# First loads, unread products and weight conversion re-ordered, and the last sums moved, in a fused retention and feed-forward kernel

## The chip, the cores and the metric

The kernel runs on one core of a Trainium2 chip. The metric is the device time in microseconds (us) of one execution, lower is better. The times given are medians of several executions; one further execution was taken with the hardware profiler on, and all rows of a profile below are from such an execution.

## The reference: what is computed

Inputs are q, k and v of shape (8 batches, 8 heads, 576 tokens, 64), in float32, and two weight matrices of 64-bit floats: w_in (512 x 2048) and w_out (2048 x 512). The output is float32, 4608 x 512.

```
scores = q @ k.T / sqrt(64)
ret    = scores * gamma_h ** (i - j)   where i >= j, else 0     (gamma_h = 1 - 2 ** (-5 - h))
attn   = ret @ v                       # per batch and head
x      = attn, heads side by side      # 4608 tokens x 512
h      = max(x @ w_in, 0)
out    = (h * h) @ w_out
```

## The kernel before, in words

**Retention.** Tokens are taken in 40 chunks, five to a batch: four of 128 tokens and one of 64. For a chunk, `turn` (L375) transposes q and k on TensorE (PE) and copies the results out with ScalarE (ACT, k) and VectorE (DVE, q); `scores` (L396) makes the products of q and k on PE, masks them on DVE (`ret`), and lets GpSimd (POOL) scale v by the decay. `retain_a`, `retain_b` and `retain_c` (L443 to L500) then make the output of the chunk and a running state u that one chunk hands to the next; the finished x of the chunk is copied by ACT into `xT`. POOL also scales the q of chunks 1 to 3 (`scale_q`, L370), in program order with the v's.

**Loads.** `load(i)` (L131) issues q, k and v of chunk i on SyncE's queue (SP): q and k in three transfers each, v in one. Chunks 0 to 2 are loaded ahead; turn i of the main loop (L708) then calls `load(i + 3)`, and in turns 0 to 3 `fetch_raw(1)` behind it, which loads one piece of w_in. One more piece is loaded ahead of the loop.

**Weight conversion.** The chip gets w_in as 64-bit words. A piece is 128 of its columns, 16 pieces in all. `round_parts` (L200) turns one into float32 in six steps: `one` and `two` on DVE (L209, L213), `beside`, two activations on ACT (L217, L218), then `three`, `four`, `five` on DVE (L221, L224, L227). The generator `w_in_parts` (L292) hands the steps out in this order: `one` and `two` of piece 0; then for each piece j: `beside` of j, `one` and `two` of j + 1, `three`, `four`, `five` of j. So six steps make one piece. `convert(n)` (L313) emits the next n steps at the place in the program where it is called; there is no scheduler, each engine runs what it is given in the order of the program.

**First block.** The feed-forward part takes 512 tokens as a block, nine in all. In block 0 the first matrix product is a plain one, `first_in(j)` (L545): four PE products of piece j with `xT` of block 0 (L553), then on ACT a ReLU of the result (L557), later a squaring on DVE (L560). `first_in(0)` and `first_in(1)` are called in turn 4 of the main loop; after that `ffn` (L668) calls three per chunk: in its first half `convert(6)` and one `first_in`, in its second half one `first_in`, `convert(6)`, another `first_in`, `convert(6)`. Blocks 1 to 8 use seven products in place of eight (`ffn_in`, L573), and from there PE has work waiting all the time.

**Unread products.** `warm` (L695) gives PE products whose results nobody reads.

**Second product.** When all tokens are through the first product, the loop over `inner` and `outer` (L824, L857) makes the second: 63 inner steps (9 blocks of 7 products), each of them again seven products of 128 x 128. DVE adds these up into `r`, and `outer` adds `r` into one or two quarters of the output and writes a half of it out when it is complete.

Of the kernel before, what the change touches and what calls it, by code (L numbers as in the profile page):

```python
# [9 lines left out]
F32 = mybir.dt.float32  # L10
# [3 lines left out]
ALU = mybir.AluOpType  # L14
# [3 lines left out]
TOK = 512  # L18
HT = TOK // 2
# [21 lines left out]
def kernel(  # L41
# [33 lines left out]
    nc = tc.nc  # L75
    ctx.enter_context(tc.manual_schedule())

    B, H, S, D = q.shape
# [9 lines left out]
    N_BLK = n_tok // TOK  # L88
    NP = len(PRODUCTS)
    NCH = -(-S // C)  # L90
    chunks = [(b, ci, ci * C, min(C, S - ci * C)) for b in range(B) for ci in range(NCH)]
    N_CH = len(chunks)
# [7 lines left out]
    ld3 = first.enter_context(tc.tile_pool(name="ld3", bufs=3))  # L100
    ld4 = first.enter_context(tc.tile_pool(name="ld4", bufs=4))
# [26 lines left out]
    loaded = {}  # L128
    N_EARLY = TOK // C

    def load(i):  # L131
        b, ci, c0, cs = chunks[i]
        got = {name: pool.tile([128, H, D], F32, tag=name, name=f"{name}_ld") for name, pool in (("q", ld3), ("k", ld4), ("v", ld4))}
        if i == 0:
            nc.sync.dma_start(dv, decay_v)
        if N_EARLY <= i < N_EARLY + NCH:

            nc.sync.dma_start(dq[:, :, c0:c0 + cs], decay_q[:, :, c0:c0 + cs])
        for name, src in (("q", q), ("k", k), ("v", v)):
            t = got[name]  # L140

            issue = nc.scalar if i == 0 and name != "q" else nc.sync
            at = src[b, :, c0:c0 + cs, :].rearrange("h s d -> s h d")
            if name == "v":
                issue.dma_start(t[:cs], at)
            else:

                issue.dma_start(t[:cs, 0:H // 2, :], at[:, 0:H // 2, :])
                for e in range(2):
                    issue.dma_start(t[:cs, H // 2 + e::2, :], at[:, H // 2 + 1 - e::2, :])  # L150
        loaded[i] = [got["q"], got["k"], got["v"]]

# [38 lines left out]
    def fetch_w(j):  # L193
        if j < len(pieces) and wide:
            nc.sync.dma_start(raw_of(j).bitcast(I64).rearrange("p (c f) -> p c f", c=N_DM), piece_src(j))
# [88 lines left out]
    def fetch_raw(count):  # L284

        for _ in range(count):
            if n_raw[0] < min(N_W1, n_made[0] + N_RAW):
                fetch_w(n_raw[0])
                n_raw[0] += 1
# [23 lines left out]
    def convert(count):  # L313
        for _ in range(count):
            f = next(w_in_steps, None)
            f and f()
# [4 lines left out]
    nc.gpsimd.memset(exp_bias, -896.0 * 2.0 ** 23)  # L321
    idle = only.tile([128, 128], F32, name="idle")
    nc.vector.memset(idle, 1.0)
    for i in range(3):
        load(i)
    fetch_raw(1)

    ident = only.tile([128, 128], F32, name="ident")
    make_identity(nc, ident)
# [3 lines left out]
    for half in range(2):  # L333
        at = slice(CH * half, CH * half + CH)
        nc.gpsimd.affine_select(
            out=msk[at, 0, 0, :], in_=msk[at, 0, 0, :], compare_op=ALU.is_ge, fill=0.0, base=0,
# [38 lines left out]
    def turn(i):  # L375

        cs, c0 = chunks[i][3], chunks[i][2]
        n_h = cs // CH
        p = ps_t.tile([128, 2, 512], F32, tag="t", name="t_ps").rearrange("p h (j d t) -> p h j d t", j=2, d=HP)
        for j in (1, 0):  # L380
            for hp in range(HP):
                for h in range(n_h):
                    nc.tensor.transpose(p[:, h, j, hp, :], loaded[i][j][rows(h), 2 * hp:2 * hp + 2, :],  # L383
                                        ident[rows(h), rows(h)])
        for j, name in ((1, "kT"), (0, "qT")):
            t = st[i][name] = work2.tile([128, HP, C], F32, tag=name, name=name) if j == 0 else work.tile([128, HP, C], F32, tag=name, name=name)
            to = t[:, :, :cs].rearrange("p d (h t) -> p h d t", h=n_h)
            if j:
                nc.scalar.copy(to, p[:, :n_h, j, :, :])
            elif i < N_EARLY:  # L390
                nc.vector.tensor_copy(to, p[:, :n_h, j, :, :])
            else:
                nc.vector.tensor_tensor(to, p[:, :n_h, j, :, :], dq[:, :, c0:c0 + cs].rearrange("p d (h t) -> p h d t", h=n_h),
                                        op=ALU.mult)
# [300 lines left out]
    def warm(count, wide):  # L695
        t = ps_f.tile([128, 512], F32, tag="f", name="idle_ps")
        for _ in range(count):
            if wide:
                nc.tensor.matmul(t[:, 0:128], lhsT=idle, rhs=idle, start=True, stop=True)
            else:  # L700
                for b in range(2):
                    nc.tensor.matmul(t[rows(b), 0:64], lhsT=idle[rows(0), rows(b)], rhs=idle[rows(0), 0:64], start=True, stop=True,  # L702
                                     skip_group_check=True)

    warm(6, True)
    scale_q(0, nc.vector)
    turn(0)
    for i in range(N_CH + 1):  # L708
        if i <= N_EARLY:

            convert((0, 0, 2, 5, 5)[i])
            if i >= 1:
                retain_a(i - 1)
                warm(4, False)
                retain_b(i - 1)
                warm(4, False)
                retain_c(i - 1)
            convert((0, 0, 1, 1, 1)[i])
            if i == N_EARLY:
                step()  # L720
            scores(i)
            if i == N_EARLY:
                convert(6)
                step()
            if i < N_EARLY:
                if i + 1 < N_EARLY:
                    scale_q(i + 1, nc.gpsimd)
                warm(6, False)
                turn(i + 1)
            else:  # L730
                convert(5)
        else:
            if i == N_EARLY + 1:
                gone[0] = TOK
            retain_a(i - 1)
            if i < N_CH:
                turn(i)
            ffn(i - 1, 0)
            retain_b(i - 1)
            if i < N_CH:  # L740
                scores(i)
            retain_c(i - 1)
            ffn(i - 1, 1)
        if i + 3 < N_CH:
            load(i + 3)
        if i < N_EARLY:
            fetch_raw(1)
    assert n_next[0] == N_BLK
# [15 lines left out]
    o_room = [part(at).rearrange("p (h j d) -> p h j d", h=2, j=2) for at in (7168, 9216)]  # L764
    N_K = N_BLK * NP
    BLOCKS = list(range(1, N_BLK)) + [0]
# [57 lines left out]
    def inner(k, i):  # L824

        n, j = divmod(k, NP)
        o = o_room[n % 2]
        if i == 0:
            small = late3.tile([128, 3, 128], F32, tag="small", name="small")
            r = o[:, 0, :, 0:HT] if j == 0 else late2.tile([128, 2, HT], F32, tag="r", name="r")  # L830
            state[k] = dict(r=r, lefts=lefts(k), p1=small[:, 0, :], u2=small[:, 1, :], p15=small[:, 2, :])
        s = state[k]
        left, right, to = PRODUCTS[i]
        if i in OPENS:
            s[to] = bank(f"o_{to}")
        p = s[to]
        for m in range(N_MQ):
            nc.tensor.matmul(p, lhsT=s["lefts"][left][:, m, :], rhs=w_out[j][:, m, WO_SLOT[right], :],  # L838
                             start=(i in OPENS and m == 0), stop=(i in CLOSES and m == N_MQ - 1),
                             skip_group_check=True)  # L840
        r = s["r"]
        if i == 0:
            nc.scalar.copy(s["p1"], p)
        elif i == 1:
            nc.vector.tensor_tensor(s["u2"], p, s["p1"], op=ALU.add)  # L845
        elif i == 2:
            nc.vector.tensor_tensor(s["p15"], p, s["p1"], op=ALU.add)
        elif i == 3:
            nc.scalar.copy(r[:, 0, 0:128], p)  # L849
        elif i == 4:  # L850
            nc.vector.tensor_tensor(r[:, 1, 128:], p, s["p15"], op=ALU.add)
        elif i == 5:
            nc.vector.tensor_tensor(r[:, 0, 128:], p, s["u2"], op=ALU.add)
        else:
            nc.vector.tensor_tensor(r[:, 1, 0:128], p, s["p1"], op=ALU.add)

    def outer(k):  # L857

        n, j = divmod(k, NP)
        r = state.pop(k)["r"]  # L860
        o = o_room[n % 2]
        c11, c12 = o[:, 0, :, 0:HT], o[:, 0, :, HT:]
        c21, c22 = o[:, 1, :, 0:HT], o[:, 1, :, HT:]
        for to, with_ in {1: [(c21, c11)], 2: [(c12, c21)], 3: [(c11, c11)], 4: [(c22, c12), (c21, c21)],
                          5: [(c12, c12)], 6: [(c21, c21)]}.get(j, []):
            nc.vector.tensor_tensor(to, r, with_, op=ALU.add)
        if j >= 5:
            half = j - 5
            row = BLOCKS[n] * TOK + half * HT
            nc.sync.dma_start(out[row:row + HT, :].rearrange("(a p) d -> p a d", p=128), o[:, half, :, :])  # L870
# [18 lines left out]
    for k in range(N_K + 1):  # L889
# [4 lines left out]
        for e in range(3):  # L894
# [8 lines left out]
            f = next(steps_0, None)  # L903
# [56 lines left out]
```

## Time and profile before

| What | us |
|---|---|
| median of 3 executions | 995.94 (995.22 to 996.46) |
| the profiled execution: its own time | 992.27 |
| the profiled execution: span from first to last instruction | 990.5 |
| PE busy | 974.3 (98% of the span) |
| DVE busy | 747.5 (75%) |
| ACT busy | 189.6 (19%) |
| POOL busy | 83.1 (8%) |
| first product of `first_in(0)` starts | 34.83 |
| last product of `first_in(15)` starts | 106.1 |
| last PE product ends | 985.6 |

Time in the profile counts from the start of the span. "PE" is the matrix product, "PEld" the loading of its stationary operand; a row of the timeline gives start, duration, engine, line, the tiles written and read with their sizes, how many instructions it merges, and in brackets how long the engine sat idle before it and what ended that.

### The profile page before, as it was taken

The numbers are of one execution on the slowest core, as the hardware profiler recorded it, in microseconds if no ns is written. First come the engines' busy times: TensorE is split into PE (matmuls) and PEld (weight loads), VectorE is DVE, ScalarE is ACT, GpSimd is POOL, SyncE is SP. The second block draws the span as 40 slices with busy tenths as digits, with TensorE's granted clock in tenths as the row PEclk, the third lists the DMA queues.
The fourth block names the chain that finished last, engine by engine and source line by source line (L and its number), as shares of the span: only waits on it lengthen the run. The fifth ranks groups of instructions, "written<-read, shape, count | busy, mean of one in ns | idle before, by whom it ended". The sixth has DMA issues, their size and how long they took to land.

```text
span 990.5 us, 24582 instructions
## 1 busy us (share of the span) xinstructions
PE 974.3 (98%) x10612; PEld 866.2 (87%) x10612; DVE 747.5 (75%) x1420; ACT 189.6 (19%) x459; POOL 83.1 (8%) x85
## 2 busy tenths in 40 slices
PE   7999999999999999999999999999999999999997
PEld 6645788888888888888888889999999999999997
DVE  2789797567878888888886777777777777776765
ACT  3455221112222222322211100000000000000000
POOL 3100011101112011110101000000000000000000
PEclk8999999999999999999999999999999999999999
DMA  8986647756796788779549999675583767556351
GB/s 190 262 235 174 184 148 200 199 139 182 206 302 215 200 261 240 219 231 269 160 180 330 406 382 349 233 268 171 214 296 138 258 207 274 192 190 237 116 202 43
DMA packets 187660, 220.40 MB, mean 223 GB/s; under 512 B 119200, under 2 KB 137632, under 8 KB 178592
## 3 DMA queue, kind: packets, MB, share of 16 engines
q1 hardware_dynamic: 185440, 218.31, 68.0%
q8 instruction: 83, 1.36, 0.6%
q10 hardware_dynamic: 2112, 0.52, 0.3%
q14 instruction: 25, 0.20, 0.1%
HBM read 129.41 MB, written 89.39 MB: 221 GB/s over the span
## 4 chain that ended last, share of the span: by engine, by line
PE 94%; DVE 4%; ACT 1%; issue 1%; DMA 0%; SPq 0%; DVEq 0%; ACTq 0%
PE o_b L838 17%; PE h_b L588 17%; PE o_c L838 11%; PE o_a L838 11%; PE h_c L588 11%; PE h_a L588 11%; PE h_ps L553 5%; PE x_ps L432 3%; PE t_ps L383 2%; PE x_ps L467 2%; PE sc_ps L411 2%; PE idle_ps L702 1%; PE u_ps L435 1%; DVE room L595 0%; DMA q_ld<-in_q_dram 0%
## 5 line engine op out<-in xcount | busy, mean ns | idle before, releaser
L588 PE MATMUL h_b<-room,w 128*128 128x256 f32 x736 | 177.2, 383 | 1.6 <-DVE room L516 0.9
L588 PEld LDWEIGHTS h_b<-room,w 128*128 128x128 f32 x736 | 137.2, 190 | 21.9 <-PE t_ps L383 1.1
L838 PE MATMUL o_b<-w,room 128*128 128x128 f32 x1168 | 144.5, 275 | 0.2 <-DVE room L789 0.2
L838 PEld LDWEIGHTS o_b<-w,room 128*128 128x128 f32 x1168 | 137.2, 192 | 0.5 <-DVE room L789 0.4
L838 PE MATMUL o_c<-w,room 128*128 128x128 f32 x1008 | 123.0, 275 | 0.0
L838 PEld LDWEIGHTS o_c<-w,room 128*128 128x128 f32 x1008 | 117.7, 192 | 0.0
L588 PE MATMUL h_c<-room,w 128*128 128x256 f32 x480 | 114.3, 381 | 0.0
L588 PE MATMUL h_a<-room,w 128*128 128x256 f32 x448 | 107.5, 383 | 0.0
L588 PEld LDWEIGHTS h_c<-room,w 128*128 128x128 f32 x480 | 90.5, 190 | 12.5
L588 PEld LDWEIGHTS h_a<-room,w 128*128 128x128 f32 x448 | 83.8, 190 | 11.8
L838 PE MATMUL o_a<-w,a 128*128 128x128 f32 x688 | 85.6, 275 | 0.0
L838 PEld LDWEIGHTS o_a<-w,a 128*128 128x128 f32 x688 | 81.2, 192 | 0.1
L605 POOL TENSOR_TENSOR room<-room 128x512 f32<-128x512 f32 x32 | 36.1, 1128 | 431.0 <-ACT room L604 361.6
L595 DVE SCALAR_TENSOR_TENSOR room<-room 128x512 f32<-128x512 f32 x96 | 67.5, 703 | 3.3
L849 ACT COPY r<-o_a 128x128 f32<-128x128 f32 x54 | 14.3, 265 | 276.9 <-PE o_a L838 246.4
L553 PE MATMUL h_ps<-room,w 128*128 128x512 f32 x128 | 58.1, 602 | 0.8 <-ACT room L489 0.7
L607 DVE TENSOR_TENSOR room<-h_b,room 128x512 f32<-128x512 f32 x32 | 22.1, 690 | 42.2 <-PE h_b L588 42.2
L432 PEld LDWEIGHTS x_ps<-ret,v_ld 64*64 64x64 f32 x1152 | 40.2, 136 | 13.3 <-issue 11.5
L432 PE MATMUL x_ps<-ret,v_ld 64*64 64x64 f32 x1152 | 49.6, 226 | 1.4 <-ACT u_sb L470 1.4
L420 POOL TENSOR_TENSOR v_ld<-v_ld,dv 128x512 f32<-128x512 f32 (+1 forms) x40 | 43.6, 1092 | 70.7 <-DMA v_ld<-in_v_dram 65.8
L845 DVE TENSOR_TENSOR small<-o_b,small 128x128 f32<-128x128 f32 x63 | 18.4, 291 | 39.4 <-PE o_b L838 39.4
L553 PEld LDWEIGHTS h_ps<-room,w 128*128 128x128 f32 x128 | 23.3, 190 | 26.7 <-issue 24.9
(102 smaller groups left out, 1385.1 us busy)
## 6 DMA issues: line engine op xcount, KB each, us to landing
g_dram<-room SPq DMA_DIRECT2D x32, 1792.0 KB, 7.3
a<-g_dram SPq DMA_DIRECT2D x43, 1024.0 KB, 7.1
room<-g_dram SPq DMA_DIRECT2D x20, 1024.0 KB, 6.2
w<-w_dram SPq DMA_DIRECT2D x7, 1792.0 KB, 12.2
out_dram<-room SPq DMA_DIRECT2D x18, 512.0 KB, 3.3
w<-in_moe_w_in_dram SPq DMA_DIRECT2D x16, 512.0 KB, 5.7
w<-in_moe_w_out_dram SPq DMA_DIRECT2D x16, 512.0 KB, 3.8
v_ld<-in_v_dram SPq DMA_DIRECT2D x31, 256.0 KB, 3.9
```

Source lines behind the costliest of these rows:

```text
L383: nc.tensor.transpose(p[:, h, j, hp, :], loaded[i][j][rows(h), 2 * hp:2 * hp + 2, :], ident[rows(h), rows(h)])
L411: nc.tensor.matmul(sc[e][rows(h), hp, :], lhsT=kT[rows(e), hp, t], rhs=qT[rows(e), hp, t], start=True, stop=True, skip_group_check=True)
L420: nc.gpsimd.tensor_tensor(vs[:cs], vs[:cs], dv[:cs, :, ci:ci + 1].to_broadcast([cs, H, D]), op=ALU.mult)
L432: own.append(lambda hp=hp, e=e, b=b: nc.tensor.matmul(x_at(hp, b, h), lhsT=s["vs"][rows(h), 2 * hp + b, :], rhs=s["ret"][rows(h), e, hp, : ...
L467: nc.tensor.matmul(x_at(hp, b, h), lhsT=u[rows(e), hp, :], rhs=s["qT"][rows(e), hp, CH * h:CH * h + CH], start=clears(b, hp // 2), stop=Fa ...
L553: nc.tensor.matmul(p.rearrange("p h t -> p (h t)"), lhsT=w[:, c, :], rhs=xT[0][:, c, :], start=(c == 0), stop=(c == N_DM - 1))
L588: nc.tensor.matmul(p[:, mm, :], lhsT=w[:, c, :], rhs=xs[n][right][:, c, :], start=(j in OPENS and mm == 0 and c == 0), stop=(j in CLOSES a ...
L595: nc.vector.scalar_tensor_tensor(t, t, 0.0, t, op0=ALU.max, op1=ALU.mult)
L605: nc.gpsimd.tensor_tensor(g["A11"], g["A11"], g["A11"], op=ALU.mult)
L607: nc.vector.tensor_tensor(g["A22"], p, p15, op=ALU.add)
L838: nc.tensor.matmul(p, lhsT=s["lefts"][left][:, m, :], rhs=w_out[j][:, m, WO_SLOT[right], :], start=(i in OPENS and m == 0), stop=(i in CLO ...
L845: nc.vector.tensor_tensor(s["u2"], p, s["p1"], op=ALU.add)
```

## The change

- `load` is split into `load_qk` and `load_v`. Turn i issues q and k of chunk i + 3, then v of chunk i + 2, then (in turns 0 to 3) a piece of w_in. Ahead of the loop the order is q0, k0, v0, q1, k1, q2, k2, v1; the piece of w_in that was loaded there is not.
- The unread products: 8 wide ones in place of 6 at the start; 20 narrow ones (`warm(10)`) behind `turn(0)`; 24 in place of 12 between `scores(0)` and `turn(1)`; none in place of 12 between `scores(i)` and `turn(i + 1)` for i = 1 to 3; 6 in place of 8 at each of the two places around `retain_b`.
- The steps of the weight conversion in turns 0 to 4: before, 3 in turn 2, 6 in turn 3 and 6 in turn 4 ahead of `first_in(0)`, 15 in all; after, 8 in turn 3 and 1 in turn 4, 9 in all. Later calls of `convert` are unchanged.
- In the last of the 63 inner steps the products are added straight into the quarter C21 of the output (`last_inner`). The additions that need no new product are made earlier, `outer` does nothing for this step, and the last half of the output leaves in two transfers of 128 rows in place of one of 256.

```diff
-    def load(i):
+    def load_qk(i):
         b, ci, c0, cs = chunks[i]
-        got = {name: pool.tile([128, H, D], F32, tag=name, name=f"{name}_ld") for name, pool in (("q", ld3), ("k", ld4), ("v", ld4))}
+        loaded[i] = [pool.tile([128, H, D], F32, tag=name, name=f"{name}_ld") for name, pool in (("q", ld3), ("k", ld4))]
...
+    def load_v(i):
+        b, ci, c0, cs = chunks[i]
+        t = ld4.tile([128, H, D], F32, tag="v", name="v_ld")
+        (nc.scalar if i == 0 else nc.sync).dma_start(t[:cs], v[b, :, c0:c0 + cs, :].rearrange("h s d -> s h d"))
+        loaded[i].append(t)
...
-    for i in range(3):
-        load(i)
-    fetch_raw(1)
+
+    load_qk(0)
+    load_v(0)
+    load_qk(1)
+    load_qk(2)
+    load_v(1)
...
-    warm(6, True)
+    warm(8, True)
     scale_q(0, nc.vector)
     turn(0)
+    warm(10, False)
     for i in range(N_CH + 1):
         if i <= N_EARLY:
 
-            convert((0, 0, 2, 5, 5)[i])
+            convert(2 if i == 3 else 0)
             if i >= 1:
                 retain_a(i - 1)
-                warm(4, False)
+                warm(3, False)
                 retain_b(i - 1)
-                warm(4, False)
+                warm(3, False)
                 retain_c(i - 1)
-            convert((0, 0, 1, 1, 1)[i])
+            convert(1 if i >= 3 else 0)
             if i == N_EARLY:
                 step()
             scores(i)
@@
             if i < N_EARLY:
                 if i + 1 < N_EARLY:
                     scale_q(i + 1, nc.gpsimd)
-                warm(6, False)
+                if i == 0:
+                    warm(12, False)
                 turn(i + 1)
+                convert(5 if i == 3 else 0)
             else:
                 convert(5)
@@
         if i + 3 < N_CH:
-            load(i + 3)
+            load_qk(i + 3)
+        if i + 2 < N_CH:
+            load_v(i + 2)
         if i < N_EARLY:
             fetch_raw(1)
@@
         r = s["r"]
-        if i == 0:
+        if k == N_K - 1:
+
+            last_inner(s, i, p)
+        elif i == 0:
             nc.scalar.copy(s["p1"], p)
@@
+    def last_inner(s, i, p):
+        n = N_BLK - 1
+        o = o_room[n % 2]
+        c21 = o[:, 1, :, 0:HT]
+        add = lambda to, x, y: nc.vector.tensor_tensor(to, x, y, op=ALU.add)
+        at = {3: (0, 0), 4: (1, 1), 5: (0, 1), 6: (1, 0)}
+        place = lambda e: c21[:, at[e][0], 128 * at[e][1]:128 * at[e][1] + 128]
+        if i == 0:
+            nc.scalar.copy(s["p1"], p)
+        elif i == 1:
+            add(s["u2"], p, s["p1"])
+            add(s["u2"], s["u2"], place(5))
+        elif i == 2:
+            add(s["p15"], p, s["p1"])
+            add(s["p15"], s["p15"], place(4))
+            add(s["p1"], s["p1"], place(6))
+        else:
+            add(place(i), p, {3: place(3), 4: s["p15"], 5: s["u2"], 6: s["p1"]}[i])
+        if i >= 5:
+            row = BLOCKS[n] * TOK + HT + (i - 5) * 128
+            nc.sync.dma_start(out[row:row + 128, :], o[:, 1, i - 5, :])
+
     def outer(k):
 
+        if k == N_K - 1:
+            return
```

More of the change, by code (lines that the diff above doesn't have):

```diff
@@ L138, in load @@
             nc.sync.dma_start(dq[:, :, c0:c0 + cs], decay_q[:, :, c0:c0 + cs])
-        for name, src in (("q", q), ("k", k), ("v", v)):
-            t = got[name]
-            issue = nc.scalar if i == 0 and name != "q" else nc.sync
+        for t, src in zip(loaded[i], (q, k)):
+            issue = nc.scalar if i == 0 and src is k else nc.sync
             at = src[b, :, c0:c0 + cs, :].rearrange("h s d -> s h d")
[L144 to L151, printed above, removed]
+            issue.dma_start(t[:cs, 0:H // 2, :], at[:, 0:H // 2, :])
+            for e in range(2):
+                issue.dma_start(t[:cs, H // 2 + e::2, :], at[:, H // 2 + 1 - e::2, :])
+    def load_v(i):
[3 more added lines that the diff above has]
+        loaded[i].append(t)
     pieces = [(0, m, e) for m in range(N_M) for e in range(2)]
```

## The prediction, made before the result was known

> **What bounds the kernel now.** I read the page first. PE is busy in 974.3 of 990.5 us, and the chain that ended last is PE for 94%: a gain can only come from the few places where PE does not run, and a new wait of PE is paid in full.
>
> ```profile
> PE 974.3 (98%) x10612; PEld 866.2 (87%) x10612; DVE 747.5 (75%) x1420; ACT 189.6 (19%) x459; POOL 83.1 (8%) x85
> PE 94%; DVE 4%; ACT 1%; issue 1%; DMA 0%; SPq 0%; DVEq 0%; ACTq 0%
> ```
>
> Such places are the first 35 us and the last 5. I cut the first with the table of stretches, along the steps of the granted clock (columns: stretch, length, busy time of PE, PEld, DVE, ACT, POOL, clock, DMA share, GB/s).
>
> ```profile
> 4.49:7.90 3.41, 0.80 (x12) 0.56 (x12) 0.84 (x2) 0.58 (x1) 0.97 (x1) 1.00 1.29 229
> 7.90:11.31 3.41, 2.82 (x65) 2.70 (x66) 1.29 (x3) 0.00 (x0) 2.04 (x3) 0.50 1.24 219
> 11.31:14.73 3.41, 3.41 (x90) 3.30 (x89) 0.69 (x1) 1.12 (x3) 1.22 (x2) 0.50 0.98 260
> 21.55:24.97 3.41, 1.89 (x67) 1.62 (x65) 0.44 (x2) 1.77 (x4) 0.00 (x0) 1.00 0.38 79
> 24.97:28.38 3.41, 3.41 (x106) 3.33 (x106) 3.34 (x6) 0.64 (x3) 1.38 (x1) 0.50 1.01 279
> 984.12:987.53 3.41, 1.46 (x14) 1.27 (x12) 1.28 (x4) 0.00 (x0) 0.00 (x0) 1.00 0.39 146
> ```
>
> A thin stretch (0.80 and 1.89 us busy) is followed by half a clock. Then comes block 0, where PE looks full. I asked for the chain of waits in 74 to 90 us, because the chain leaves PE there (start, length, what):
>
> ```profile
> 75.75 3.65 PE h_ps L553 x8
> ...
> 79.42 0.60 ACT room L557
> 80.01 0.61 ACT w L217
> 80.62 0.57 ACT w L218
> ...
> 81.22 0.70 DVE w L221
> ...
> 81.94 1.46 DVE w L224
> ...
> 83.42 0.70 DVE w L227
> 84.13 0.04 issue
> 84.17 3.70 PE h_ps L553 x8
> ```
>
> The reader is to see a loop: the end of one product of block 0 releases its ReLU on ACT; behind the ReLU in ACT's order stand the two conversion steps of a piece; behind them three DVE steps; behind these a product of block 0. Products 9, 10 and 11 start at 75.68, 79.22 and 84.17. The ReLU that opens the loop is that of product 9, the piece that ends it is for product 11, and product 10 (3.6 us) lies beside it. PE loses nothing only because conversion is one piece ahead. The end of the span, in the timeline:
>
> ```profile
> 985.62 0.29 DVE L855 TENSOR_TENSOR r<-o_b,small 128x128 f32<-128x128 f32 x1 [0.60 <-PE o_b L838]
> 986.01 0.69 DVE L866 TENSOR_TENSOR room<-r,room 128x512 f32<-128x512 f32 x1
> ```
>
> [...] 1.89 us of small products lost the clock, while 1.46 us of dense ones, at the end, kept it. [...] L217 follows at once on L557 although its input was long there. [...] L224 takes 0.69 us, but 1.43 to 1.53 where a POOL multiplication runs.
>
> **The weight conversion, the largest part.** Before, 15 steps are emitted ahead of `first_in(0)`: 2 + 6 x 2 + 1, so pieces 0 and 1 are done. After, 9: 2 + 6 + 1, only piece 0. All later calls are unchanged, so every later step stands one piece later in DVE's and ACT's order; the built program shows it: 2 + 3 DVE instructions and 2 on ACT are gone from the start and stand at the end of the conversion. The work is the same; its lead is gone. Product j now waits for a piece whose ACT steps stand behind the ReLU of product j - 1. Loop time from the start of the ReLU to the end of L227: 79.42 to 84.11 is 4.69 us; the same reading in three other turns gives 4.49 (52.38 to 56.87), 3.94 (65.78) and 3.96 (93.14); mean 4.27, with hand-overs of 0.03 and 0.05 some 4.3. What stands between the two products on PE decides:
> - Products 4, 7, 10, 13 follow directly on 3, 6, 9, 12. Nothing covers the loop: 4 x 4.3 = 17.2.
> - Products 5, 8, 11, 14 follow on a `retain_a` and a `turn`, which took 55.77 to 57.05, 1.28 us: 4 x (4.3 - 1.3) = 12.0.
> - Product 1: on DVE its piece now stands behind the mask of chunk 4, which waits for scores that PE makes after product 0. The same DVE row of work ran from 39.19 to 43.44, beside product 1; now in front of it: 4.2.
> - Products 2, 3, 6, 9, 12, 15: their piece is converted beside the product before. 0.
>
> Sum +33.4. Bounds: with L224 always at 0.69, 4 x 4.0 + 4 x 2.7 + 3.5 = 30.3; always at 1.46, 4 x 4.75 + 4 x 3.45 + 4.2 = 37.0. Queued behind a waiting product on PE are the next chunk's retention and scores, and behind these ACT and DVE: nothing fills the gap, and as PE has work to the end, nothing gives it back.
>
> **The clock in those gaps.** Nine gaps of 3 to 4.3 us in windows of 3.41. A dense product at half clock takes 3.63 more; a lost window costs at most 1.7. No row shows such gaps between dense products. From below: 0, since 1.46 busy us of dense ones kept the clock. From above: each gap trips and often a second window stays slow, about 10 windows, +17. I take half of the nine: 5 x 1.7, +8.
>
> **The start, up to the first product of block 0 (34.83).**
> - Unread products. Narrow ones at full clock take 0.69 us per 12. The 20 behind `turn(0)` fill 7.1 to 8.45, where PE waits for the copies of k and q: no cost, and they can hold the clock. From scores to scores, chunk 0 takes 6.97 us (8.50 to 15.47) and chunk 1 5.09 (15.47 to 20.56); full clock can give about 1.9, and 12 more unread products take 0.7 back: -1.2. Chunks 1 to 3 lose 12 products each, 3 x 0.7; their cover is the mask on DVE (0.76), which `retain_a` awaits and of which the transposes (0.65) hide most: -0.5 each, -1.5. The 8 to 6: the one ahead of `retain_b` only covers ACT's copy of u, 0; the other -0.12 each, -0.5.
> - Loads. v1 moves behind six issues of q2 and k2 on SP, at 0.52 each from the timeline, 3.1 us: landing, worked out from issue times and the landing events, from 10.35 to about 13.4. POOL is in order: v1 (1.06), then q2 (1.06), ready at 15.5 in place of 12.7. `turn(2)` ran at 16.57 before; the cover is 1 us, and what the other edits gain above that is given back here, some +1. v2, raw pieces and q3 stand later or earlier by one place; DMA moves some 220 to 260 GB/s here either way. v3 and later are issued a chunk later; a chunk of block 0 takes 13 us against some 4 for a landing: 0.
> - Two "issue" stalls of PE (1.52 at 22.05, 0.93 at 31.57) [...]: -0.8, open.
>
> Sum -3.0; bounds -5 (no second dip of the clock either) and +1 (v1 late, stalls longer). Piece 0 is then ready about when ACT has copied x, so nothing more is won.
>
> **The end.** Behind the last product stand 0.29 + 0.69 us of DVE, a transfer and its landing. After: one addition of 0.29, and 128 rows in place of 256. The new additions of 0.29 fall in gaps of DVE of 0.60 us: 0. The 0.69 and its hand-over go, -0.75, and a smaller transfer may give 0.3: -1.0, bounds -0.7 and -1.6.
>
> **Sum.** +33.4 + 8 - 3.0 - 1.0 = +37. The profiled execution's own 992.27 becomes 1029.3; it lies 3.67 below the median of the runs. The sum is a difference, so I add it to the median: 995.94 + 37 = 1033.
>
> **Rivals.**
> - Half the gaps lose the clock (forecast): 1033, 0.50.
> - The stalls, but no clock loss, as at the end of the trace: +33.4 - 4 = +29, 1025. For it: products of block 0 are dense. 0.20.
> - Nearly every gap loses the clock, as 1.89 us of 3.41 did at 24.97: +33.4 + 17 - 4 = +46, 1042; with L224 long, 1046. 0.23.
> - Not slower: the lead of one piece was not needed, because ACT's steps get in ahead of the ReLU and conversion runs beside the product. Then only start and end count: -4, 992. It decides where the loop is at most what PE does between: 0 us for product 4, 1.3 for product 5, against 3.9 measured. Against it: the order of ACT in the built program, ReLU of product 3, then the steps of piece 4. 0.07.
>
> **Range.** Low: -5 + 30.3 + 0 - 1.6 = +23.7, 1019.6. High: +1 + 37.0 + 17 - 0.7 = +54.3, 1050.2. It leaves out the last rival and some tails. A measurement of this kernel can tell about 0.2% from no change. Faster 0.06, same 0.01, slower 0.93.
>
> **What would show it.** PE sits idle ahead of the h_ps products about 30 us in nine gaps, put down to DVE; block 0 (34.83 to 106.1 before, 71) lasts over 100. Dips of the clock inside it tell the second from the third case. Block 0's first product at about 32. Last PE product to the end shorter by 1. Wrong: products 3 and 4 back to back as before.

## The result, and the profile after

The changed kernel takes **1039.19 us** (median of 4 runs, 1034.84 to 1040.2); the kernel before, beside it on the same chip, 995.98 us (995.22 to 996.46). The ratio is 1.0426, 95% interval 1.0395 to 1.0458: slower. The profiled execution took 1040.2 us, its span is 1038.5 us, 48.0 longer than that of before. That is more than the 43.2 us between the medians, since the profiled execution of before lies 3.7 below its median; the stages below are those of these two executions.

I read the two traces stage by stage. Three stages of each make the difference (us); what lies between the second and the third is 878.9 us in both:

| | before | after | difference |
|---|---|---|---|
| start of the span to the first product of block 0 | 34.83 | 38.23 | +3.4 |
| from there to the end of block 0's last product (product 15) | 71.85 | 117.88 | +46.0 |
| last addition of the last product to the end of the span | 4.92 | 3.42 | -1.5 |

The page of after, its busy times, the clock by slices, the chain that ended last and the row of block 0's products (the row counts PE's instructions; a product of block 0, numbered 0 to 15 below, is eight of them):

```profile
PE 992.2 (96%) x10576; PEld 872.8 (84%) x10576; DVE 745.4 (72%) x1423; ACT 189.1 (18%) x458; POOL 83.5 (8%) x85
...
PEclk9988889999999999999999999999999999999999
...
PE 90%; DVE 6%; ACT 2%; issue 1%; DMA 0%; SPq 0%; DVEq 0%; ACTq 0%
...
L557 PE MATMUL h_ps<-room,w 128*128 128x512 f32 x128 | 73.6, 728 | 31.4 <-DVE w L228 30.7
```

The same row of before:

```profile
L553 PE MATMUL h_ps<-room,w 128*128 128x512 f32 x128 | 58.1, 602 | 0.8 <-ACT room L489 0.7
```

PE's share of the chain fell from 94% to 90%; DVE and ACT took most of it. The loss has two parts. PE sat idle for 30.7 us ahead of `h_ps`, until the last conversion step of a piece. And PE was busy 18 us longer (992.2 against 974.3) with fewer products: its clock was lower in slices 3 to 6 (8 tenths, where before has 9). The stage alone, in the table of stretches, first before, then after:

```profile
34.83:106.68 71.85, 71.68 (x762) 36.51 (x764) 59.23 (x99) 33.75 (x68) 6.47 (x6) 1.00 0.80 219
```

```profile
38.23:156.11 117.88, 87.22 (x762) 41.34 (x764) 60.37 (x104) 34.57 (x70) 7.16 (x6) 0.87 0.46 129
```

Both have 762 instructions on PE: the busy time of PE grew by 15.5 us with no work added. The rest of the stage, 117.88 - 87.22 = 30.7 us, is idle PE, where before it was 0.2. So +46.0 = 30.5 + 15.5.

The loop in the chain of waits of after, around product 4:

```profile
57.92 3.02 PE h_ps L557 x7
...
60.97 0.60 ACT room L561
61.56 0.61 ACT w L218
62.17 0.55 ACT w L219
...
62.74 0.70 DVE w L222
...
63.47 0.70 DVE w L225
...
64.19 0.70 DVE w L228
...
64.94 6.75 PE h_ps L557 x8
```

It is the loop that the prediction showed in 79.42 to 84.11 of before, with the same ReLU, the same two ACT and three DVE steps. But it now ends in the product that follows directly on the one that began it: nothing lies beside it, PE waits 4.02 us. ACT's order shows in it: what L218 reads was written by 53.84 (L210 on DVE, 53.42 + 0.42), ACT sat idle for 3.24 us ahead of the ReLU at 60.97, and L218 ran behind the ReLU all the same, at 61.46 in ACT's timeline. And that product then takes 6.75 us in place of 3.70. Why, the table of stretches shows, cut along the steps of the clock. Each row is one window of 3.41 us: all steps of the clock in this trace lie on one grid, from 23.30 to 149.59 us 37 windows of 3.413 each. The column after POOL is the granted clock (1.00 full, 0.50 half):

```profile
60.84:64.26 3.42, 0.09 (x1) 0.00 (x0) 1.45 (x3) 1.75 (x3) 0.00 (x0) 1.00 0.00 0
64.26:67.67 3.41, 2.73 (x4) 1.18 (x5) 1.90 (x4) 0.00 (x0) 0.00 (x0) 0.50 0.41 95
67.67:71.08 3.41, 3.41 (x6) 1.35 (x4) 0.00 (x0) 0.00 (x0) 0.00 (x0) 0.50 0.98 365
71.08:74.50 3.42, 1.87 (x50) 1.13 (x48) 0.97 (x2) 2.78 (x6) 0.00 (x0) 1.00 0.00 1
74.50:77.91 3.41, 2.21 (x5) 1.06 (x6) 3.34 (x7) 0.89 (x2) 0.00 (x0) 1.00 0.28 68
```

The gap of product 4 fills a window (0.09 us busy), and two at half clock follow. Product 4 spends 6.14 of its 6.75 us in these; an instruction of it takes up to 1061 ns between 67.67 and 71.08, and 592 in products at full clock. The gap of product 5, 2.74 us from 72.95 to 75.69, is split over two windows (1.87 and 2.21 us busy) and costs no clock. Eight of the nine gaps lost it, one of them for two windows: nine windows at half.

The end, in the timeline of after:

```profile
1035.06 0.29 DVE L873 TENSOR_TENSOR room<-o_b,small 128x128 f32<-128x128 f32 x1 [0.60 <-PE o_b L847]
1035.38 0.33 SPq L889 DMA_DIRECT2D out_dram<-room  x1
```

From the last addition to the issue of the transfer 0.32 us where it was 1.11, and from there to the end 3.10 where it was 3.81.

### The profile page after: what moved, and what is told of

It is laid out like the page before. It is cut to its first block, busy times and chain, and to the rows that moved or that the text cites. A ratio compares the mean times of both kernels' runs of the same rounds, so it can differ in the third digit from the quotient of the medians.

```text
span 1038.5 us, 24492 instructions
## 1 busy us (share of the span) xinstructions
PE 992.2 (96%) x10576; PEld 872.8 (84%) x10576; DVE 745.4 (72%) x1423; ACT 189.1 (18%) x458; POOL 83.5 (8%) x85
## 4 chain that ended last, share of the span: by engine, by line
PE 90%; DVE 6%; ACT 2%; issue 1%; DMA 0%; SPq 0%; DVEq 0%; ACTq 0%
PE o_b L847 16%; PE h_b L592 15%; PE o_c L847 11%; PE o_a L847 11%; PE h_c L592 10%; PE h_a L592 10%; PE h_ps L557 7%; PE x_ps L436 3%; PE t_ps L387 2%; PE x_ps L471 2%; PE sc_ps L415 2%; DVE w L228 1%; DVE w L222 1%; PE idle_ps L706 1%; DVE w L225 1%
## 5 line engine op out<-in xcount | busy, mean ns | idle before, releaser
L557 PE MATMUL h_ps<-room,w 128*128 128x512 f32 x128 | 73.6, 728 | 31.4 <-DVE w L228 30.7
L557 PEld LDWEIGHTS h_ps<-room,w 128*128 128x128 f32 x128 | 28.3, 232 | 67.6 <-issue 35.5
L222 DVE SCALAR_TENSOR_TENSOR w<-w,w 128x512 f32<-128x512 uint32 x32 | 21.9, 686 | 38.1 <-ACT w L219 37.9
```

The costliest lines, as they stand in the source:

```text
L222: nc.vector.scalar_tensor_tensor(t, bits, 2.0 ** -20, as_dst(j, frac), op0=ALU.mult, op1=ALU.add)
L557: nc.tensor.matmul(p.rearrange("p h t -> p (h t)"), lhsT=w[:, c, :], rhs=xT[0][:, c, :], start=(c == 0), stop=(c == N_DM - 1))
```

## The experiments

My theory: conversion lost its lead, so two ACT steps of each piece stand behind the ReLU of the product before; the gaps trip the clock. The rival: the loads or the unread products slow the start and block 0, and conversion is only where it shows. A second question was the start, which came later where I had forecast earlier. Times beside each other are from the same chip; ratios are against the kernel before.

**The lead given back.**

```diff
-            convert(1 if i >= 3 else 0)
+            convert((0, 0, 0, 1, 7)[i])
```

> The changed kernel with one thing undone: the six conversion steps (piece 1 of w_in) are again emitted ahead of the first product of block 0; loads, unread products and last sums stay changed. Theory (the lead of the conversion is the cause): the 46.0 us by which block 0 grew go, PE's idle time ahead of h_ps falls from 31.4 to under 2 us, no half-clock window lies in block 0, and what stays is the later start and the shorter end, +3.4 - 1.4: about 998 us. Rival (later loads of v or the unread products slow block 0): still about 1039 us, with the gaps still there.

Measured 994.32 us against 994.55, ratio 0.9995 (0.9981 to 1.0009). The row of block 0's products in its page:

```profile
L557 PE MATMUL h_ps<-room,w 128*128 128x512 f32 x128 | 58.1, 602 | 1.9 <-DVE w L228 1.9
```

Gaps and lost clock are gone with this one edit: block 0 lasts 71.85 us, as in before, without a half-clock window (no instruction of its products takes over 697 ns, as in before). The 998 us expected were too many: the later start of the single profile was not in the median.

**The lead taken from the kernel before.**

```diff
-            convert((0, 0, 2, 5, 5)[i])
+            convert(2 if i == 3 else 0)
...
-            convert((0, 0, 1, 1, 1)[i])
+            convert(1 if i >= 3 else 0)
...
+                convert(5 if i == 3 else 0)
```

> The kernel before with one thing changed: its conversion calls are those of the changed kernel, nine steps ahead of block 0 in place of fifteen. Theory: gaps of 31 us ahead of h_ps and nine half-clock windows at 1.7 us each, +46: about 1042 us; perhaps a little less, as fewer conversion steps stand in DVE's way at the start. If the lost clock came from another edit, only the gaps: 996 + 31 = 1027 us. Rival (the lead is not needed): 996 us.

Measured 1040.99 us, ratio 1.0456 (1.0419 to 1.0493): +45.4 us.

```profile
L553 PE MATMUL h_ps<-room,w 128*128 128x512 f32 x128 | 73.7, 729 | 31.4 <-DVE w L227 30.7
```

The same 30.7 us of waits as in the changed kernel, and a mean of 729 ns where that has 728, with loads, unread products and end as before. Taking the lead away is enough to bring the loss, and giving it back is enough to remove it; the rival falls.

**One step of lead.** What is it about the lead? The run differs from the changed kernel by a single conversion step.

```diff
-            convert(1 if i >= 3 else 0)
+            convert((0, 0, 0, 1, 2)[i])
```

> The changed kernel with one conversion step more ahead of block 0, ten in place of nine: the two ACT instructions of every later piece stand ahead of the ReLU of the product before in ACT's order in place of behind it; the DVE steps keep their places but for one. Theory (the cost is the place of two ACT instructions behind a ReLU, not the sixth of a piece or the amount of work): the gaps of products 4, 5, 7, 8, 10, 11, 13 and 14 go, with their half-clock windows; product 1 may keep its gap of about 4 us and one window, as its piece stays behind a mask on DVE: about 995 to 1002 us, ratio 1.000 to 1.008. Rival (a whole piece of lead is needed, each step worth a sixth of the 46 us): about 1033 us, ratio 1.038.

Measured 1002.46 us, ratio 1.0070 (1.0043 to 1.0097). One step of six brings 35 of the 42 us. So most of the cost is no matter of amount: it is the place of two ACT instructions of 0.7 us behind or ahead of a ReLU in ACT's queue, which was worked in order here (61.46 behind 60.97 above). What stays, in its chain of waits around product 1:

```profile
40.08 0.64 PE sc_ps L415 x16
...
40.74 0.68 DVE ret L422
41.42 0.33 DVE w L214
41.75 0.61 DVE w L222
...
43.12 0.70 DVE w L228
...
43.95 1.10 PE h_ps L557 x2
```

Piece 1 stays behind the mask of chunk 4, which waits for scores. Product 1 waits 3.27 us for it; all waits of this kernel for DVE ahead of block 0's products are 7.4 us, the other 4.1 in six waits of 0.3 to 1.4.

**The gaps filled.** Unread wide products in the nine gaps; the waits stay as they were. A wide one is a full 128 x 128 product; a narrow one, further below, is a pair of 64 x 64.

```diff
+        if j % 3 == 1:
+            warm(15, True)
+        elif j % 3 == 2 and j > 2:
+            warm(10, True)
```

> The changed kernel with unread wide products put on PE in the nine gaps, 15 ahead of products 1, 4, 7, 10 and 13 and 10 ahead of products 5, 8, 11 and 14; nothing else changed, the waits stay. Theory (the gaps trip the clock, at 1.7 us for each half-clock window): the half-clock windows of block 0 go, the waits of about 31 us stay though PE looks busy in them: 15 us less, ratio about 1.0275 against before, some 1022 us. Rival 1 (the lost clock has another cause, so the windows stay): 1.042 as before, or more. Rival 2 (unread products outlast the gaps): the waits are covered but PE's own work grows, above 1.03.

Measured 1027.26 us, ratio 1.0309 (1.0286 to 1.0332), 11 to 12 us less than the changed kernel. PE is given 115 unread products more to do (230 instructions in the trace, 246 with those at the start), and the kernel gets faster:

```profile
L561 PE MATMUL h_ps<-room,w 128*128 128x512 f32 x128 | 60.6, 618 | 5.6 <-DVE w L228 4.9
L707 PE MATMUL idle_ps<-idle 128*128 128x128 f32 x246 | 31.4, 287 | 1.1 <-DVE idle L324 1.1
```

The mean instruction of block 0's products takes 618 ns, not 728. One product is slower, the first, ahead of all nine gaps: it takes 5.40 us (from 36.43), and the products behind the gaps 3.67, as at full clock; the mean clock of the stage is 0.98, one window's worth below 1.00. So none of the nine gaps loses the clock, and that the gaps tripped it is shown. The gain is 3 us short of the 15 expected, and the ratio is also what rival 2 had. The slow first product is 1.7 of it, and eight of the gaps last 0.1 us longer each than in the changed kernel; the rest is open.

**The loads alone**, on the kernel before: v behind the next chunks' q and k, and no piece of w_in ahead of the loop (the diff of the change, lines of `load_qk` and `load_v`).

> The kernel before with only the loads changed: v behind the next chunks' q and k, and no piece of w_in loaded ahead of them; conversion, unread products and end as before. Theory A (the loads made the start of block 0 3.4 us later): first product of block 0 at about 38 us in place of 34.8, total about 999 us. Theory B (the unread products did it, by the clock): first product at 34 to 35.5 us, total 996 us, within 1 us. As piece 1 of w_in is fetched later here while its conversion stands where it stood, a wait for it may add up to 3 us.

Measured 996.91 us, ratio 1.0021 (1.0007 to 1.0035): 2.1 us slower, between the two theories. Its profile has the first product at 38.67 us, which alone would fit theory A. But that start is not the same in all executions: the profile of the kernel with only its end changed, whose start is that of before, has 35.9 us where before has 34.83, and an instruction of block 0's products takes up to 1223 ns in it, 697 in before: the clock was lost at other places. So a start read from one profile is uncertain by 1.1 us at least, a third of the 3.4 in question.

Which part of the loads? The same, with the first piece of w_in loaded ahead of the loop as before:

```diff
     load_v(1)
+    fetch_raw(1)
```

> The kernel before with only v's loads moved behind the next chunk's q and k; the first piece of w_in is loaded ahead of the chunks' loop as before. It tells which edit of the loads costs the 2.1 us (ratio 1.0021) that both together cost. Theory A (the late v1, which POOL has to scale before q2): ratio 1.002. Theory B (each piece of w_in is fetched one chunk later): ratio 1.000.

Measured 995.91 us against 995.88, ratio 0.9999 (0.9980 to 1.0018). That speaks for theory B, the late pieces of w_in, but the two intervals overlap: not settled.

**The unread products alone**, on the kernel before.

```diff
-    warm(6, True)
+    warm(8, True)
...
+    warm(10, False)
...
-                warm(4, False)
+                warm(3, False)
...
-                warm(4, False)
+                warm(3, False)
...
-                warm(6, False)
+                if i == 0:
+                    warm(12, False)
```

> The kernel before with only the unread products changed (8 wide at the start, 10 and 12 narrow ones in chunk 0, 3 in place of 4 in the chunks after, the 6 ahead of each turn gone). Theory from the run with the lead given back: that run had the changed loads (ratio 1.0021 alone), the changed end (0.9986 alone) and these products, and came to 0.9995; so these should give about 0.9988, some 1.2 us faster: 993.4 us where before is 994.6. Rival (the 20 added narrow ones cost what the dropped ones give): ratio 1.000. My forecast's term for these products alone was -3.2 us: 0.9968.

Measured 993.87 us against 995.04, ratio 0.9988 (0.9975 to 1.0000): -1.2 us, not the -3.2 of my forecast. The rival's 1.000 is the edge of the interval.

**The end alone** (`last_inner` of the diff, on the kernel before).

> The kernel before with only the last inner sums made on C21 and the last rows sent by quarters. Theory: the stretch from the last addition on DVE to the end of the span is 1.5 us shorter, all else the same: 996.0 - 1.5 = 994.5 us, ratio 0.9985. Rival (the additional additions hold back PE's last products, so the gain is given back): 996 us, ratio 1.000.

Measured 993.88 us against 994.55, ratio 0.9986 (0.9970 to 1.0002): -1.4 us by the ratio, as the trace has it, though the interval just takes in 1.

**The two parts that seem to pay**, together: unread products and end of the change, loads and conversion of before.

> The kernel before with the two parts of the change that seem to pay: the changed unread products and the changed end; loads and conversion as before. Theory (the parts add): 0.9986 x 0.9988, ratio about 0.9974, some 992.0 us where before is 994.6. Rival (one of the two gains was chance): 0.9985 to 1.000.

Measured 992.99 us against 995.04, ratio 0.9973 (0.9958 to 0.9989). The parts add, and together they are faster than both kernels, with an interval below 1. Its start still has a long stretch at half clock:

```profile
4.14:7.55 3.41, 2.02 (x38) 1.59 (x39) 0.69 (x1) 0.47 (x2) 0.56 (x1) 1.00 1.21 229
7.55:10.96 3.41, 3.41 (x87) 3.41 (x84) 1.45 (x3) 0.13 (x1) 2.15 (x3) 0.50 1.05 211
10.96:14.38 3.42, 3.42 (x79) 3.19 (x78) 0.26 (x1) 0.58 (x1) 1.51 (x2) 0.50 0.56 122
14.38:17.79 3.41, 3.41 (x108) 3.37 (x103) 0.44 (x1) 1.12 (x4) 1.06 (x1) 0.50 1.17 292
```

From 7.55 on PE is busy in every microsecond, mostly with narrow unread products and scores up to 12.3, and the clock comes back only at 17.79, after three windows.

**Wide in place of narrow.** In that kernel `warm(10)` and `warm(12)` of chunk 0 become 6 and 7 wide ones.

```diff
-    warm(10, False)
+    warm(6, True)
...
-                    warm(12, False)
+                    warm(7, True)
```

> As the kernel before with changed unread products and changed end, but the 10 and 12 narrow unread products of chunk 0 are 6 and 7 wide ones of about the same length. In that kernel's trace the clock is at half from 7.6 to 17.8 us although narrow products and scores fill PE for much of it. Theory (dense products on the whole array restore the clock in a window in which small ones don't): full clock comes one or two windows of 3.41 us earlier, at 11 to 14.5 us, and the kernel gains 1.7 to 3: ratio 0.994 to 0.9956. Rival (what counts is that PE is busy, not with what): clock and time as there, ratio 0.9973.

Measured 990.91 us against 995.88, ratio 0.9959 (0.9942 to 0.9977), the fastest of all, though the interval takes in the 0.9973 of the rival too: the time alone does not decide. In its trace the clock is full from 5.78 to 29.67 us, where that of the kernel with narrow ones is at half from 7.55 to 17.79.

**All of them wide.**

```diff
-                warm(3, False)
+                warm(2, True)
...
-                warm(3, False)
+                warm(2, True)
```

> The kernel with 6 and 7 wide unread products in chunk 0, the changed end and the loads and conversion of before; now the 3 narrow unread products in each half of a retention in the chunks after are 2 wide ones too. In that kernel's trace the clock is full from 5.8 to 29.7 us and at half from there to 36.5. Theory (dense unread products hold the clock): no half-clock window from about 6 us up to the end of block 0, first product of block 0 at 32 us or earlier: another 0.5 to 2 us, ratio 0.994 to 0.9955. Rival [...]: half-clock windows at some place of the start all the same, ratio 0.996 or above.

Measured 991.08 us against 994.49, ratio 0.9968 (0.9955 to 0.9981). The clock did the first half of what the theory said: it was full from 5.30 to 46.26, and the first product of block 0 came at 31.0 us. But then a half-clock window lies in block 0, as the rival had it, and the ratio is the rival's too. Block 0 of this kernel and of the one before it:

```profile
31.00:106.98 75.98, 73.25 (x762) 37.46 (x762) 60.43 (x102) 33.66 (x68) 6.85 (x6) 0.98 0.80 219
```

```profile
32.60:106.42 73.82, 73.55 (x762) 37.27 (x764) 59.33 (x99) 33.76 (x68) 6.77 (x6) 0.97 0.83 223
```

It starts 1.6 us earlier and ends 0.6 later, with 2.7 us of idle PE in place of 0.3: in its waits DVE stands 3.3 us for pieces of w_in to land, in those of the other kernel not at all in this stretch. The windows around the longest stop:

```profile
42.85:46.26 3.41, 1.11 (x19) 0.33 (x17) 3.34 (x7) 1.80 (x4) 0.00 (x0) 1.00 1.06 359
46.26:49.68 3.42, 3.42 (x50) 2.62 (x51) 3.35 (x7) 0.37 (x1) 0.00 (x0) 0.50 1.20 312
```

There PE waits 2.30 us for a copy of `turn` on DVE, which stands in DVE's order behind the conversion of a piece that landed late. The lost window follows on this gap, as those of the changed kernel follow on theirs. The earlier start is given back to the loads, in idle time and in clock.

## Why the prediction was right, and where not

**The lead of the conversion, +33.4.** Right in mechanism, place and nearly in size: 30.7 us in nine gaps. Products 4, 7, 10 and 13 waited 4.02 each (forecast 4.3), 5, 8, 11 and 14 waited 2.75 (3.0), product 1 3.60 (4.2). The difference is two DVE steps: each of the three takes 0.70 us in the loop of after, while of the four turns in my mean one had 1.46 for L224 and one 1.24 for L221, each beside a POOL multiplication (at 81.79 and 53.81); my lower bound, with 0.69 throughout, was 30.3. The two runs that give the lead back (1.0426 to 0.9995) and take it away (1.0456) put its whole effect, clock included, at 43 and 45 us, and the single step shows that the order on ACT carries most of it.

**The clock, +8.** The mis-sized term: it measured 15.5. The step that failed is "I take half of the nine" (and 5 x 1.7 is 8.5, not 8). I had set against the loss that 1.46 busy us in a window kept the clock, and the table of before has that: the 2.97 us behind it, to the end of the span, read 1.00, though no product lies in them. But a gap of 4.0 us, even when it is split evenly over two windows, leaves no more than 1.4 in each, and these four were not split so: windows with 0.09, 0.00, 0.00 and 0.00 us busy belong to products 4, 7, 10 and 13. The gaps of 2.75 and 3.6 us lost the clock four times of five, with 0.68 to 1.05 us busy. Nor were they nine draws: from product 7 to 10, and from 10 to 13, it is 23.88 us, and 7 windows of 3.413 us are 23.89, so gaps of one kind lie alike in the windows. The kernel before without its lead lost as much: 729 ns for an instruction of these products, 728 in after. Each window cost 15.5 / 9 = 1.7, as forecast. In block 0 of after the windows with 0 to 1.05 us busy were lost and those with 1.87 and 2.21 us kept. That is no bound for other stretches: at the start 1.89 us busy lost the clock in before (21.55 to 24.97), and 2.57 us in the kernel with wide unread products further above (26.26 to 29.67). So the rival with nearly every gap losing the clock (+46 in all, waits included) had the right count of lost windows, and my likeliest case the wrong one. That the sum still came near was in part luck: 2.7 us of waits too many stood in for clock.

**The start, -3.0.** Wrong. The parts measured alone give +2.1 for the loads (I had +1; POOL took v1 and then q2 in the trace of after, at 14.22 and 15.24, so q2 was ready at 16.30 where I had 15.5) and -1.2 for the unread products (I had -3.2), so about +0.9; the +3.4 of the profile is one execution. The step that failed: the narrow products "can hold the clock". A narrow instruction takes 311 ns in the half-clock windows of before and 218 at full clock. With the changed unread products alone in the kernel before, its mean was 268 ns (184 of them), where the 224 of before have 248: a larger part of them ran at half. Not all of that is theirs: with only the loads changed, and the 224 narrow ones of before, the mean was 264. In the trace of after 311 ns lasts up to 16.48, though the clock column reads 1.00 there too, and from there it is 218, which is part of the +3.4. In three traces with narrow products in chunk 0, full clock came, or came back, at 14.73 (before), 16.48 (after) and 17.79 (unread products and end changed); in the two with wide ones it held from 5.78 and 5.30 on, up to 29.67 and 46.26. That only the kind of product makes the difference is not shown: the windows lie elsewhere in each trace (a step of the clock at 7.90 in before and one at 16.48 in after are 2.5 windows apart), and two traces are few. The stalls of PE put down to "issue", an estimate of -0.8 in the forecast, stayed open: one of 3.16 us (at 19.47) stands in the trace of after where the longest of before is 1.52.

**The end, -1.0.** The profile has -1.5, the run of this part alone -1.4. The addition and its hand-over were 0.8 of it (forecast 0.75); the smaller transfer 0.7, where I allowed 0.3.

**The sum.** 45.4 + 2.1 - 1.2 - 1.4 = 44.9 us from the parts alone, each with its own interval; measured together 1.0426, 42.4 us (39.3 to 45.6). The parts add, within what can be told. The forecast of 37 was the sum of a clock term 7.5 too small, a start 3.9 too good, waits 2.7 too large and an end 0.4 too weak: -7.5 - 3.9 + 2.7 + 0.4 = -8.3, so 45.3. The two parts that pay are worth 1.2 and 1.4 us; the lost lead costs 43 to 45.

## What to carry to other kernels

A conversion that runs beside the products needs a lead, and here the lead counted in places of the queues, not in work (one step of six brought 35 of 42 us): before moving steps, write down for each piece what stands ahead of it on each engine, and whether that waits for the product just before its user. Price a gap of PE twice, once as idle time and once by what it leaves busy in a window of the clock: here windows with up to 1.05 us busy of 3.41 were lost, at 1.7 us each. Parts of a change that pay and parts that cost should be run alone: here two small gains, clear of noise only when taken together, stood behind a loss some seventeen times their sum.

## What the runs showed of the hardware that was not expected

- Making PE do unread work in its gaps won 12 us: with 115 wide products added the stage of block 0 is 105.8 us, without them 117.88.
- Being busy was not enough to get the clock back: 3.41 and 3.42 us of narrow and small products, in 7.55 to 14.38 of the kernel with unread products and end changed, left it at half, though a third such window (14.38 to 17.79) restored it, and one in the kernel before (11.31 to 14.73) did so too. The eight windows with 3.08 to 3.41 us of dense products in block 0 of after restored it (3.08 in 88.15 to 91.56), one with 2.73 did not (64.26 to 67.67).
- Three kernels with the same loads and unread products (the changed one, and those with six and with one step of lead given back) started block 0 at 38.2, 35.7 and 34.2 us, the one with the fewest conversion steps ahead of it last: a start read from one profile says little about edits of 1 us.
